# Pair 0 of the second layer's tail woven one step sooner with its operations held in order, and the last pair's bank copies put ahead of the softmax operations of the pair before it

## The chip, the cores and the metric

One core of one Trainium2 chip. The metric is device time in microseconds (us) of one execution, the median of several runs. Engines are called PE (TensorE, matrix products), DVE (VectorE), ACT (ScalarE), POOL (GpSimd) and SP (SyncE, here it only issues DMA). L937 is line 937 of the kernel before.

## The reference

Three stages, of which the last one carries the change:

```python
# stage 1: retention; x is 3072 tokens x 512
state = gamma * state + einsum('bhd,bhe->bhde', k[t], v[t])
y[t] = scale * einsum('bhd,bhde->bhe', q[t], state)
# stage 2: 512 -> 2048 -> 512
h = x @ w_in;  x = (h - tanh(h)) @ w_out
# stage 3: 512 -> 1024 -> 512
h = x @ w_in2
e = exp(h - max(h));  solu = h * e / (sum(e) + 1e-9)
ln = (solu - mean(solu)) / sqrt(var(solu) + 1e-6) * g_ln
return ln @ w_out2
```

## The kernel before, in words

Matrix products run on operands split into a high and a low part (`h`, `l`; `uh`, `ul` and so on): a 32-bit value is rounded to the format that PE takes at full rate (a cast on ACT), and the rest is what DVE or POOL get by subtraction. Each product is then three matmuls: high by high, high by low, low by high.

The end of stage 2 is a loop over `steps`, pairs (s, f): s counts six blocks of 512 tokens, f the 16 slices of 128 hidden features. Each step is 12 matmuls into four banks (`products_y`, L382), and two steps ahead of its use `split_p` casts the input `gp` on ACT (L165) and subtracts on DVE (L166). During the last block, s = 5, work of stage 3 for its first tokens is woven in between the steps.

Stage 3 takes 24 tiles of 128 tokens in 12 pairs. The first product of a pair, `h = x @ w_in2`, is done in seven block products instead of eight (`P1, P2, P6, P5, P7, P4, P3`, in this order; `Pair.part`, L1037): six matmuls each (`product2`, L930), with sums of the inputs made ahead (`sum_y` on POOL, `split_y`: casts `yha` and `yhs` on ACT, L508, subtractions `yla`, `yls` on POOL, L480). Some products add into a bank that an earlier one has filled, after the earlier sum has been copied out: P6 and P7 go on in P1's bank, P3 in P5's. `keep2` (L937, ACT) is that copy, four for each pair (after P1, P6, P5 and P7), and the bank can't be written on before the copy has been read out. `add_half` (L945, DVE) adds a bank and a kept copy into half a row of h and keeps the running minimum of -h.

Then for each half of the pair (`sa`, done first, and `sb`), class `Soft`: `exp` (L958, ACT), `weigh` (L964, DVE: h times e, and its mean), `center` (L970, ACT: less the mean), `turn` (L974, DVE: transposition in blocks, then a DMA to DRAM, L975) and `norm` (L980, ACT: Square with its sum, then small DVE and POOL operations). The function `turn(j)` reads both halves back with tokens and features exchanged (L992, SP). `high` (L999, ACT) and `low` (L1003, DVE) split that, and `outp` (L1015) makes the output tile: 24 matmuls, of which the first eight take `uh` alone, then a copy times the scale (L1028, ACT) and a DMA out. `outs(j)` does both tiles of pair j, tile 2j+1 (half a) first.

The order of PE in the tail is the program's own (`manual_schedule`). Other instructions are put in order by a scheduler, and those that pass through `fix` are held to the program's order once `late[0]` is true. Before the change that is so from the tail on; in the weave it is false. In the tail, pair j's seven products run (`pair_of`), and `high` and `low` of pair j-1 stand between the parts; for pair 1 they stand elsewhere (L1133 to L1166). Pair 10 is not followed by `outs`: its softmax runs, then its two `norm`, then pair 11's products, then the outputs of pairs 9, 10 and 11.

Of the kernel before, what the change touches and what calls it, by code (L numbers as in the profile page):

```python
# [43 lines left out]
NSB = NC  # L44
# [45 lines left out]
def body(ctx: ExitStack, tc, z, w_in, w_out, w_in2, w_out2, g_ln, cst, tab, out):  # L90
# [9 lines left out]
    def pin(ins, on=True):  # L100

        if on:
            tc.keep_in_program_order(ins)

    def t4(shape, dtype, name):
        return big.tile(shape, dtype, tag="t4", name=name)
# [51 lines left out]
    P1, P2, P6, P5, P7, P4, P3 = range(7)  # L158
    late = [False]

    def fix(ins):
        pin(ins, late[0])
# [303 lines left out]
    def step2(m):  # L466
        for st, n in enumerate((m + 3, m + 2, m + 1, m)):
            dec2.to(st, n)


    def load_y(j):
        t = t4([P, 2, NK, P], F32, "yl")
        nc.sync.dma_start(out=t, in_=y1d[j // 2][:, j % 2 * 2 : j % 2 * 2 + 2, :, :])
        yl[j] = t
# [196 lines left out]
    for n in range(NF1):  # L671
# [16 lines left out]
        else:  # L688

            dec1.n = 2 * NF1  # L690
            m = n - (NF1 - 4)
# [104 lines left out]
    def y_banks(s):  # L796
        at = [(ps_h, "h")] * 4 if s % 2 else [(ps_a, "r"), (ps_a, "r"), (ps_h, "h"), (ps_h, "h")]
        py[:] = [pool.tile([P, SB], F32, tag=tag, name="py") for pool, tag in at]

    def load_g(upto):  # L800
        while len(gs) < min(upto, len(steps)):
            s, f = steps[len(gs)]
            t = t2([P, SB], F32, "g")
            nc.sync.dma_start(out=t, in_=gd[s][:, f, :])
            gs[s, f] = t

    def split_p(n):
        w = t4([P, 2, SB], F32R, "gp")
        parts(w[:, 0, :], w[:, 1, :], gs[steps[n]], nc.vector)
        gp[n] = (w[:, 0, :], w[:, 1, :])  # L810
# [3 lines left out]
    def load_wo(upto):  # L814
        while len(wof) < min(upto, NF1):
            f = len(wof)
            wof[f] = t2([P, 512], F32, "wf")
            nc.sync.dma_start(out=wof[f], in_=wod[f])

    def split_wo(f):  # L820
        wo[f] = stage3(wof[f], None, nc.vector, False)
# [18 lines left out]
    for n in range(len(q) + 1):  # L840
        now, was = n < len(q), n > 0
        p, j = q[n] if now else (NSB, 0)
# [76 lines left out]
    def bank2():  # L919
        pool, tag = bank_of[0]  # L920
        bank_of.append(bank_of.pop(0))
        return pool.tile([P, 512], F32, tag=tag, name="ph2")

    def product2(j, m, ph, first=True):
        a = ys[j][m]
        n = 0
        for r in range(2):
            bh, bl = com.w[m, r]
            for x, w in ((a[0], bh), (a[0], bl), (a[1], bh)):
                nc.tensor.matmul(  # L930
                    ph, x[:, r, :], w, start=first and n == 0, stop=n == 5, skip_group_check=True
                )
                n += 1

    def keep2(ph):
        t = t2([P, 512], F32, "part")
        fix(nc.scalar.copy(t, ph))  # L937
        return t
# [4 lines left out]
    def add_half(h, half, ph, part, seen):  # L943
        hn, nm = h
        fix(nc.vector.tensor_tensor_reduce(  # L945
            hn[:, half * 512 : (half + 1) * 512], ph, part, -1.0,
            3.0e38 if seen is None else nm[seen], ALU.add, ALU.min, nm[half],
        ))

    class Soft:  # L950
# [21 lines left out]
        def turn(self):  # L972
            t = t4([P, FF2], F32, "ut")
            fix(nc.vector.transpose(t, self.hn))  # L974
            pin(nc.sync.dma_start(out=ud[self.i], in_=t))  # L975
            uc[self.i] = self.hn
# [20 lines left out]
    def high(i):  # L997
        uh, ul = ut[i] = [t4([P, NF2 * P], F32R, "u" + n) for n in "hl"]
        fix(nc.scalar.copy(uh, uc[i]))  # L999

    def low(i):
        uh, ul = ut[i]
        fix(nc.vector.tensor_tensor(ul, uc.pop(i), uh.bitcast(F32), ALU.subtract))  # L1003
# [27 lines left out]
    class Pair:  # L1031
# [5 lines left out]
        def part(self, m):  # L1037
            j = self.j
            if m == P1:
                self.q1 = bank2()  # L1040
                product2(j, P1, self.q1)
                self.kept = keep2(self.q1)
            elif m == P2:
                q = bank2()
                product2(j, P2, q)
                add_half(self.b, 0, q, self.kept, None)
            elif m == P6:
                product2(j, P6, self.q1, False)
                self.u2 = keep2(self.q1)
            elif m == P5:  # L1050
                self.q3 = bank2()
                product2(j, P5, self.q3)
                self.p5 = keep2(self.q3)
            elif m == P7:
                product2(j, P7, self.q1, False)
                self.kept = keep2(self.q1)
                add_half(self.a, 1, self.q1, self.p5, None)
            elif m == P4:
                q = bank2()
                product2(j, P4, q)  # L1060
                add_half(self.a, 0, q, self.kept, 1)
                self.sa = Soft(2 * j + 1, self.a, 0)
                self.sa.exp()
            else:
                product2(j, P3, self.q3, False)
                add_half(self.b, 1, self.q3, self.u2, 0)
                self.sb = Soft(2 * j, self.b, 1)
                self.sb.exp()
                ys.pop(j)

    bank_of = []
# [2 lines left out]
        nc.sync.dma_start(out=gd[s][:, f, :], in_=g)  # L1074
    for n, (s, f) in enumerate(steps):
        if n:
            if f == 0:
                y_banks(s)
                if s == NSB - 1:
                    bank_of[:] = [(ps_a, "r"), (ps_a, "r"), (ps_h, "h"), (ps_h, "h")]  # L1080
            load_g(n + 5)
            load_wo(n + 4)
            if n + 2 < len(steps):
                split_p(n + 2)
            if n + 2 < NF1:
                split_wo(n + 2)
            products_y(f, gp.pop(n), wo[f], py)
        if f == NF1 - 1:
            keep_y(s, py)
        if s >= NSB - 3 and n % 2 == 0 and com.n[2] < 12:  # L1090
            com.step()
        m = n - 2 * NF1 - 6
        if m >= 0 and m % 3 == 0:
            step2(m // 3)
        if s == NSB - 1:
            if f == 0:
                load_y(0)
            if f == 2:
                sum_y(0)
                load_y(1)  # L1100
            if f == 4:
                split_y(0)
            if f == 6:
                sum_y(1)
            if f == 9:
                load_y(2)
            if f == 8:
                pair = Pair(0)
            for m in {8: (P1, P2), 9: (P6, P5), 10: (P7, P4), 11: (P3,)}.get(f, ()):
                pair.part(m)  # L1110
                if m in (P4, P3):
                    u = pair.sa if m == P4 else pair.sb
                    u.weigh()
                    u.center()
                    u.turn()
                    u.norm()
            if f == 9:
                split_y(1)
            if f == 11:
                sum_y(2)  # L1120
            if f == 12:
                turn(0)
    G.close()
    M.close()

# [3 lines left out]
    NJ = NTT // 2  # L1129
# [3 lines left out]
    def pair_of(j, before=None):  # L1133

        a, b = (None, None) if before is None else (2 * before + 1, 2 * before)
        pair = Pair(j)
        for n, m in enumerate((P1, P2, P6, P5, P7, P4, P3)):
            pair.part(m)
            if n < 2 and j + 1 < NJ:
                split_y(j + 1, (n,))  # L1140
            if n == 2 and a is not None and j > 1:
                high(a)
                low(a)
            if n == 4:
                if a is not None:
                    if j > 1:
                        high(b)
                    else:
                        high(a)
                        low(a)  # L1150
                if j + 2 < NJ:
                    sum_y(j + 2)
                if j + 3 < NJ:
                    load_y(j + 3)
        for u in (pair.sa, pair.sb):
            u.weigh()
        if a is not None and j == 1:
            high(b)
        pair.sa.center()
        pair.sa.turn()  # L1160
        if a is not None:
            low(b)
        pair.sb.center()
        pair.sb.turn()
        turn(j)
        return pair  # L1166

    def outs(j, of=None, after=None):
# [8 lines left out]
    late[0] = True  # L1177
    with tc.manual_schedule(engines={mybir.EngineType.PE}):
        for j in range(1, NJ - 2):
            pair = pair_of(j, j - 1)  # L1180
            outs(j - 1, pair)
        pair = pair_of(NJ - 2, NJ - 3)
        pair.sa.norm()
        pair.sb.norm()
        pair = pair_of(NJ - 1)
        outs(NJ - 3, pair, NJ - 2)
        outs(NJ - 2, None, NJ - 1)
        outs(NJ - 1)
# [59 lines left out]
```

## Time and profile before

| | |
|---|---|
| three runs | 860.66 us median (860.16 to 861.43) |
| the profiled execution, its own time | 864.85 us |
| its span, first to last instruction | 863.1 us |
| PE busy | 823.6 us, 95% of the span |
| DVE, ACT, POOL busy | 64%, 55%, 36% |
| the weave of pair 0 (s = 5, f = 8 to 15) | 578 to 614.5 us |
| the tail, pairs 1 to 11 and all outputs | 614.5 to 860 us |
| mean granted clock of PE | 0.98 |

A busy PE is counted from modelled ends, so a matmul of 128x512 lasts 0.39 us in a row while the next one starts 0.227 us after it. In a timeline a row is a run of like instructions: start, duration, engine, line, operation, tiles, count, and in brackets how long the engine had been idle before it and what ended that.

### The profile page before, as it was taken

Reading aid. Unit: us, or ns where it says so; the run is one execution under the profiler, and the core shown is the slowest. Engines: PE = TensorE matmul, PEld = TensorE weight load, DVE = VectorE, ACT = ScalarE, POOL = GpSimd, SP = SyncE. Lnnn points to the kernel's source line nnn. Section 1 sums busy time; section 2 is a strip of 40 time slices with the busy share of each in tenths; the row PEclk is TensorE's granted clock in tenths of the full one; section 3 lists DMA queues with packets and bytes.
Section 4 is the critical chain, followed back from the end, with each engine's and each line's share of the span. In section 5 each row is a group of like instructions: output and inputs, shape, how many; then the busy total and the mean of one; then the engine's idle time right before and its main releaser. Section 6 shows DMA issues by size and latency. Waiting matters only on the chain.

```text
span 863.1 us, 16439 instructions
## 1 busy us (share of the span) xinstructions
PE 823.6 (95%) x6296; PEld 676.4 (78%) x6296; DVE 551.9 (64%) x1000; ACT 470.7 (55%) x880; POOL 309.0 (36%) x304
## 2 busy tenths in 40 slices
PE   4799999999999999999999999999899999999798
PEld 4678788788877777888888888887778888888686
DVE  3788875999856958232572888474466566565551
ACT  4555743656455546444571537254477677676652
POOL 4511200090534339443400260153545455455300
PEclk9799999999999999999999999999999999999999
DMA  9658753343898825964592718461877777777782
GB/s 360 251 198 308 260 197 131 122 175 122 301 363 303 304 76 170 403 256 142 199 373 86 285 57 302 140 233 37 160 146 147 147 147 147 161 165 142 128 147 62
DMA packets 168606, 169.43 MB, mean 196 GB/s; under 512 B 105680, under 2 KB 118224, under 8 KB 168528
## 3 DMA queue, kind: packets, MB, share of 16 engines
q1 hardware_dynamic: 160176, 153.51, 59.3%
q10 hardware_dynamic: 8352, 14.87, 4.9%
q8 instruction: 49, 0.80, 0.4%
q14 instruction: 29, 0.24, 0.1%
HBM read 107.02 MB, written 61.34 MB: 195 GB/s over the span
## 4 chain that ended last, share of the span: by engine, by line
PE 72%; DVE 11%; DMA 6%; issue 5%; ACT 4%; POOL 1%; SPq 1%; ACTq 0%; DVEq 0%; POOLq 0%
PE py L382 20%; PE po L1015 14%; PE ph L758 13%; PE ph L930 12%; PE ph L357 8%; DMA z<-z 3%; PE out L233 2%; PE sc L233 2%; DVE gl L373 1%; DVE wf L142 1%; DVE wf L145 1%; DVE w L155 1%; DMA raw<-w_in 1%; DMA gd<-hs 1%; DVE wf L139 1%
## 5 line engine op out<-in xcount | busy, mean ns | idle before, releaser
L382 PE MATMUL py<-gp,w 128*128 128x512 f32 x768 | 177.7, 392 | 2.5 <-ACT gp L165 2.1
L382 PEld LDWEIGHTS py<-gp,w 128*128 128x128 f32 x768 | 145.1, 189 | 34.1 <-ACT gp L165 2.8
L1015 PE MATMUL po<-w,uh 128*128 128x512 f32 x384 | 106.6, 389 | 0.0
L776 POOL TENSOR_TENSOR hs<-hs,th 128x512 f32<-128x512 f32 x48 | 66.7, 1393 | 95.6 <-ACT th L774 85.4
L1015 PEld LDWEIGHTS po<-w,uh 128*128 128x128 f32 x384 | 72.1, 188 | 15.0
L357 PE MATMUL ph<-xh,w 128*128 128x512 f32 x256 | 83.3, 400 | 0.1
L382 PE MATMUL py<-gh,w 128*128 128x512 f32 x256 | 79.2, 390 | 0.3 <-ACT gh L370 0.3
L154 ACT CAST w<-wf 128x512 fp32r<-128x512 f32 x70 | 43.0, 620 | 57.0 <-DVE wf L145 47.3
L930 PE MATMUL ph<-w,yhs 128*128 128x512 f32 x192 | 61.4, 402 | 4.9 <-ACT part L937 4.9
L1015 PE MATMUL po<-w,ul 128*128 128x512 f32 x192 | 63.1, 390 | 0.9 <-DVE ul L1003 0.9
L774 ACT ACTIVATE th<-hs 128x512 f32<-128x512 f32 x48 | 30.3, 632 | 61.2 <-DVE hs L784 54.7
L155 DVE TENSOR_TENSOR w<-wf,w 128x512 fp32r<-128x512 f32 x70 | 51.8, 745 | 14.5 <-ACT w L154 13.6
L166 DVE TENSOR_TENSOR gp<-g,gp 128x512 fp32r<-128x512 f32 x64 | 48.8, 774 | 19.1 <-ACT gp L165 19.0
L758 PE MATMUL ph<-xh,wch 128*128 128x512 f32 x140 | 56.9, 406 | 1.9 <-DVE hs L784 1.6
L945 DVE CUSTOM_DVE_ANT_0 hn<-ph,part 128x512 f32<-128x512 f32 x24 | 16.6, 692 | 64.9 <-ACT yha L508 41.5
L357 PEld LDWEIGHTS ph<-xh,w 128*128 128x128 f32 x256 | 48.6, 190 | 11.4 <-DVE w L155 0.6
L784 DVE TENSOR_TENSOR hs<-ph,part 128x512 f32<-128x512 f32 x48 | 33.0, 687 | 37.4 <-PE ph L758 24.0
L382 PEld LDWEIGHTS py<-gh,w 128*128 128x128 f32 x256 | 48.0, 188 | 10.6 <-ACT gh L370 0.7
L758 PE MATMUL ph<-xh,wcl 128*128 128x512 f32 x140 | 54.9, 392 | 1.1 <-issue 1.1
L165 ACT CAST gp<-g 128x512 fp32r<-128x512 f32 x64 | 38.6, 617 | 31.4 <-DMA g<-gd 21.4
L758 PE MATMUL ph<-xl,wch 128*128 128x512 f32 x140 | 54.9, 392 | 0.0
L758 PE MATMUL ph<-xh,wc 128*128 128x512 f32 x168 | 52.8, 390 | 0.3 <-ACT part L768 0.3
(125 smaller groups left out, 1794.1 us busy)
## 6 DMA issues: line engine op xcount, KB each, us to landing
z<-z SPq DMA_DIRECT2D x48, 512.0 KB, 7.1
g<-gd SPq DMA_DIRECT2D x64, 256.0 KB, 5.4
raw<-w_in SPq DMA_DIRECT2D x24, 512.0 KB, 6.6
raw<-w_out SPq DMA_DIRECT2D x24, 512.0 KB, 4.4
gd<-hs SPq DMA_DIRECT2D x48, 256.0 KB, 3.7
ud<-ut SPq DMA_DIRECT2D x24, 512.0 KB, 3.2
hn<-ud SPq DMA_DIRECT2D x24, 512.0 KB, 6.8
y1d<-ysb SPq DMA_DIRECT2D x24, 256.0 KB, 3.7
```

What stands on the lines that cost most here:

```text
L154: pin(nc.scalar.copy(hi, wf), fixed)
L155: pin(eng.tensor_tensor(lo, wf, hi.bitcast(F32), ALU.subtract), fixed)
L165: fix(nc.scalar.copy(h, src))
L166: fix(eng.tensor_tensor(o, src, h.bitcast(F32), ALU.subtract))
L233: pin(nc.tensor.matmul(o, a, b, start=True, stop=True, skip_group_check=True), held[0])
L357: nc.tensor.matmul(ph, a[:, k, :], x, start=n == 0, stop=n == 3 * NK - 1), s < 2
L382: nc.tensor.matmul(py[e], a[:, cols], x, start=f == 0 and n == 0, stop=f == NF1 - 1 and n == 2)
L758: nc.tensor.matmul(ph, a, x, start=first and n == 0, stop=n == 5, skip_group_check=True)
L776: eng.tensor_tensor(g, h, th, ALU.subtract)
L784: nc.vector.tensor_tensor(h, ph, part, ALU.add)
L930: nc.tensor.matmul(ph, x[:, r, :], w, start=first and n == 0, stop=n == 5, skip_group_check=True)
L1015: nc.tensor.matmul(po, a[:, f, :], dec2.w[f][lo], start=n == 0, stop=n == len(todo) - 1)
```

## The change

- In the last block, `late[0]` becomes true at f = 6, so what passes through `fix` is held in order from there.
- Pair 0's seven parts move from f = 8 to 11 to f = 7 to 10. Its softmax is no longer done half by half at once: at f = 10 stand weigh a, exp b, center a and turn a; at f = 11 weigh b, center b, turn b and the read-back; norm a at f = 12, norm b at f = 13. `exp` of half b leaves `Pair.part`.
- Pair 1 takes `high` and `low` of pair 0 at the same places as later pairs: half a behind P6, `high` of half b behind P7, `low` of half b behind its own turn a.
- The softmax of pair 10 is spread over the parts of pair 11: behind P1 weigh a, exp b, center a; behind P2 turn a, weigh b; behind P6 center b, turn b and the read-back; behind P5 norm a; behind P7 norm b. `low` of pair 9's half b moves ahead of pair 10's weigh.

```diff
@@ class Pair @@
                 self.sb = Soft(2 * j, self.b, 1)
-                self.sb.exp()
                 ys.pop(j)
@@ the loop over steps @@
         if n:
+            late[0] = late[0] or s == NSB - 1 and f == 6
...
-            if f == 8:
+            if f == 7:
                 pair = Pair(0)
-            for m in {8: (P1, P2), 9: (P6, P5), 10: (P7, P4), 11: (P3,)}.get(f, ()):
+            for m in {7: (P1, P2), 8: (P6, P5), 9: (P7, P4), 10: (P3,)}.get(f, ()):
                 pair.part(m)
-                if m in (P4, P3):
-                    u = pair.sa if m == P4 else pair.sb
-                    u.weigh()
-                    u.center()
-                    u.turn()
-                    u.norm()
+            if f == 10:
+                pair.sa.weigh()
+                pair.sb.exp()
+                pair.sa.center()
+                pair.sa.turn()
+            if f == 11:
+                pair.sb.weigh()
+                pair.sb.center()
+                pair.sb.turn()
+                turn(0)
+            if f == 12:
+                pair.sa.norm()
+            if f == 13:
+                pair.sb.norm()
             if f == 9:
                 split_y(1)
             if f == 11:
                 sum_y(2)
-            if f == 12:
-                turn(0)
@@ pair_of @@
-            if n == 2 and a is not None and j > 1:
+            if n == 2 and a is not None:
                 high(a)
                 low(a)
             if n == 4:
                 if a is not None:
-                    if j > 1:
-                        high(b)
-                    else:
-                        high(a)
-                        low(a)
+                    high(b)
...
+            yield n, pair
+        if j < NJ - 2:
+            pair.sb.exp()
+            pair.sa.weigh()
+            pair.sb.weigh()
+            pair.sa.center()
...
+        elif a is not None:
             low(b)
@@ the tail @@
-        pair = pair_of(NJ - 2, NJ - 3)
-        pair.sa.norm()
-        pair.sb.norm()
-        pair = pair_of(NJ - 1)
+        of = whole(NJ - 2, NJ - 3)
+        for n, pair in pair_of(NJ - 1):
+            if n == 0:
+                of.sa.weigh()
+                of.sb.exp()
+                of.sa.center()
+            elif n == 1:
+                of.sa.turn()
+                of.sb.weigh()
+            elif n == 2:
+                of.sb.center()
+                of.sb.turn()
+                turn(NJ - 2)
+            elif n == 3:
+                of.sa.norm()
+            elif n == 4:
+                of.sb.norm()
+        pair.sb.exp()
+        pair.sa.weigh()
...
         outs(NJ - 3, pair, NJ - 2)
```

Three places show how the built programs differ. The first is DVE in the weave, before (`ex_6793`, `hn_6686` are half a of pair 0, `ex_6844`, `hn_6689` half b; `gp_6814` is the input of f = 13, `gp_6868` that of f = 14):

```order
L974 STREAM_TRANSPOSE ut_6800<-hn_6686 128x1024
L983 TENSOR_SCALAR ssq_6803<-ssq_6803,ssum_6794 128x1
L984 TENSOR_SCALAR ssq_6803<-ssq_6803 128x1
L166 TENSOR_TENSOR gp_6814<-g_6709,gp_6814 128x512
L964 SCALAR_TENSOR_TENSOR ex_6844,us_6847<-hn_6689,ex_6844 128x1024
L981 TENSOR_SCALAR ssum_6845<-ssum_6845 128x1
L967 TENSOR_SCALAR us_6847<-us_6847 128x1
L982 RECIPROCAL ssum_6845<-ssum_6845 128x1
L974 STREAM_TRANSPOSE ut_6851<-hn_6689 128x1024
L983 TENSOR_SCALAR ssq_6854<-ssq_6854,ssum_6845 128x1
L984 TENSOR_SCALAR ssq_6854<-ssq_6854 128x1
L166 TENSOR_TENSOR gp_6868<-g_6759,gp_6868 128x512
```

and with the change (half a is `ex_6762`, `hn_6659`, half b `ex_6806`, `hn_6662`; `gp_6781`, `gp_6815`, `gp_6852` are the inputs of f = 12, 13, 14):

```order
L166 TENSOR_TENSOR gp_6781<-g_6682,gp_6781 128x512
L945 ISA hn_6662,nm_6664<-ph2_6717,part_6715,nm_6663 128x512
L945 ISA nm_6664 128x1
L964 SCALAR_TENSOR_TENSOR ex_6762,us_6803<-hn_6659,ex_6762 128x1024
L967 TENSOR_SCALAR us_6803<-us_6803 128x1
L964 SCALAR_TENSOR_TENSOR ex_6806,us_6838<-hn_6662,ex_6806 128x1024
L967 TENSOR_SCALAR us_6838<-us_6838 128x1
L974 STREAM_TRANSPOSE ut_6810<-hn_6659 128x1024
L166 TENSOR_TENSOR gp_6815<-g_6726,gp_6815 128x512
L974 STREAM_TRANSPOSE ut_6842<-hn_6662 128x1024
L166 TENSOR_TENSOR gp_6852<-g_6779,gp_6852 128x512
L981 TENSOR_SCALAR ssum_6763<-ssum_6763 128x1
```

The gp subtraction of f = 13 stood behind half a's whole chain and ahead of weigh b; now it stands behind both weighs and turn a, ahead of turn b, and the small operations of `norm` come after that of f = 14.

The second is ACT in the weave, before (names as above; `yha` and `yhs` are pair 1's inputs):

```order
L937 COPY part_6734<-ph2_6692 128x512
L937 COPY part_6743<-ph2_6736 128x512
L937 COPY part_6782<-ph2_6692 128x512
L958 ACTIVATE ex_6793,ssum_6794<-hn_6686,nm_6687 128x1024
L970 ACTIVATE hn_6686<-ex_6793,us_6796 128x1024
L980 ACTIVATE ex_6793,ssq_6803<-ex_6793,us_6796 128x1024
L165 CAST gp_6814<-g_6709 128x512
L958 ACTIVATE ex_6844,ssum_6845<-hn_6689,nm_6691 128x1024
L970 ACTIVATE hn_6689<-ex_6844,us_6847 128x1024
L980 ACTIVATE ex_6844,ssq_6854<-ex_6844,us_6847 128x1024
L165 CAST gp_6868<-g_6759 128x512
L165 CAST gp_6885<-g_6812 128x512
```

and now:

```order
L958 ACTIVATE ex_6762,ssum_6763<-hn_6659,nm_6660 128x1024
L508 CAST yha_6765<-yl_6541 128x512
L508 CAST yha_6765<-yl_6541 128x256
L508 CAST yhs_6772<-ysum_6637 128x1024
L165 CAST gp_6781<-g_6682 128x512
L958 ACTIVATE ex_6806,ssum_6807<-hn_6662,nm_6664 128x1024
L970 ACTIVATE hn_6659<-ex_6762,us_6803 128x1024
L165 CAST gp_6815<-g_6726 128x512
L970 ACTIVATE hn_6662<-ex_6806,us_6838 128x1024
L165 CAST gp_6852<-g_6779 128x512
L980 ACTIVATE ex_6762,ssq_6867<-ex_6762,us_6803 128x1024
L165 CAST gp_6876<-g_6813 128x512
```

The casts of gp stood behind exp, center and Square of a half; now one of them stands behind nearly every piece, and both Squares come last. Pair 1's three y casts moved behind exp a.

The third is ACT at the last pair, before (`ph2_8784` is the bank of P1, P6 and P7 of pair 11, `ph2_8809` that of P5 and P3; `ex_8730` and `ex_8740` are half a and b of pair 10):

```order
L958 ACTIVATE ex_8730,ssum_8731<-hn_8652,nm_8653 128x1024
L958 ACTIVATE ex_8740,ssum_8741<-hn_8655,nm_8657 128x1024
L970 ACTIVATE hn_8652<-ex_8730,us_8743 128x1024
L970 ACTIVATE hn_8655<-ex_8740,us_8746 128x1024
L980 ACTIVATE ex_8730,ssq_8760<-ex_8730,us_8743 128x1024
L980 ACTIVATE ex_8740,ssq_8769<-ex_8740,us_8746 128x1024
L937 COPY part_8791<-ph2_8784 128x512
L937 COPY part_8807<-ph2_8784 128x512
L937 COPY part_8816<-ph2_8809 128x512
L937 COPY part_8824<-ph2_8784 128x512
```

and now (the banks are `ph2_8747` and `ph2_8791`, half b is `ex_8759`):

```order
L958 ACTIVATE ex_8730,ssum_8731<-hn_8652,nm_8653 128x1024
L937 COPY part_8754<-ph2_8747 128x512
L958 ACTIVATE ex_8759,ssum_8760<-hn_8655,nm_8657 128x1024
L970 ACTIVATE hn_8652<-ex_8730,us_8756 128x1024
L937 COPY part_8783<-ph2_8747 128x512
L970 ACTIVATE hn_8655<-ex_8759,us_8774 128x1024
L937 COPY part_8798<-ph2_8791 128x512
L980 ACTIVATE ex_8730,ssq_8800<-ex_8730,us_8756 128x1024
L937 COPY part_8815<-ph2_8747 128x512
L980 ACTIVATE ex_8759,ssq_8818<-ex_8759,us_8774 128x1024
```

The four copies stood behind all six softmax operations of pair 10; now the first stands behind exp a alone, the second behind exp b and center a, the third behind center b, the fourth behind the first Square.

## Rows read from the trace of the kernel before

**Rows 1.** Waits of PE from 560 us to the end: engine, line, waited for, total us, times, longest.

```profile
PE ph L930 <- ACT part L937: 4.9, 1, 4.9
...
PE po L1015 <- DVE ul L1003: 0.9, 1, 0.9
```

**Rows 2.** Timeline of PE in the weave: start, us, engine, line, operation, count, idle before.

```profile
598.55 3.30 PE L382 MATMUL py<-gp,w 128*128 128x512 f32 x13
...
606.97 0.51 PE L382 MATMUL py<-gp,w 128*128 128x512 f32 x1 [2.06 <-ACT gp L165]
607.69 7.01 PE L382 MATMUL py<-gp,w 128*128 128x512 f32 x23 [0.22 <-DVE gp L166]
614.54 0.62 PE L930 MATMUL ph<-w,yha 128*128 128x512 f32 x2
```

**Rows 3.** Windows: stretch, busy of PE, PEld, DVE, ACT, POOL, then granted clock, DMA share, GB/s.

```profile
608.00:610.00 2.00, 2.00 (x6) 1.52 (x6) 1.38 (x2) 0.00 (x0) 1.42 (x3) 0.50 1.09 211
...
818.00:820.00 2.00, 2.00 (x6) 1.52 (x6) 0.37 (x2) 0.38 (x1) 0.00 (x0) 0.50 1.13 202
```

**Rows 4.** Timeline of ACT in the weave.

```profile
583.43 0.93 ACT L508 CAST yha<-yl 128x512 fp32r<-128x512 f32 x2
...
585.21 0.62 ACT L165 CAST gp<-g 128x512 fp32r<-128x512 f32 x1
...
595.57 1.15 ACT L958 ACTIVATE ex<-hn,nm 128x1024 f32<-128x1024 f32 x1 [1.67 <-DVE nm L945]
...
606.31 1.12 ACT L165 CAST gp<-g 128x512 fp32r<-128x512 f32 x2
```

**Rows 5.** Timeline of PE at the last pair.

```profile
808.86 0.62 PE L930 MATMUL ph<-w,yha 128*128 128x512 f32 x2
...
816.65 1.22 PE L930 MATMUL ph<-w,yhs 128*128 128x512 f32 x2 [4.91 <-ACT part L937]
...
826.36 1.98 PE L1015 MATMUL po<-w,uh 128*128 128x512 f32 x8
```

**Rows 6.** Timeline of ACT at the last pair.

```profile
808.60 1.15 ACT L958 ACTIVATE ex<-hn,nm 128x1024 f32<-128x1024 f32 x1 [0.28 <-DVE nm L945]
...
811.39 1.15 ACT L970 ACTIVATE hn<-ex,us 128x1024 f32<-128x1024 f32 x1 [0.23 <-DVE us L967]
...
816.03 0.56 ACT L937 COPY part<-ph 128x512 f32<-128x512 f32 x1
```

**Rows 7.** Timeline of DVE with POOL idle, in block s = 5 and at the last pair.

```profile
561.78 0.69 DVE L166 TENSOR_TENSOR gp<-g,gp 128x512 fp32r<-128x512 f32 x1 [0.62 <-ACT gp L165]
...
809.06 0.75 DVE L945 CUSTOM_DVE_ANT_0 hn<-ph,part,nm 128x512 f32<-128x512 f32 x1 [0.50 <-PE ph L930]
...
809.87 1.23 DVE L964 SCALAR_TENSOR_TENSOR ex<-hn,ex 128x1024 f32<-128x1024 f32 x1
...
811.21 1.22 DVE L964 SCALAR_TENSOR_TENSOR ex<-hn,ex 128x1024 f32<-128x1024 f32 x1
...
812.57 1.25 DVE L974 STREAM_TRANSPOSE ut<-hn 128x1024 f32<-128x1024 f32 x1
813.74 1.18 DVE L1003 TENSOR_TENSOR ul<-hn,uh 128x1024 fp32r<-128x1024 f32 x1
```

**Rows 8.** Timeline of DVE, with POOL at work, in the weave and in pair 2.

```profile
569.74 1.22 DVE L166 TENSOR_TENSOR gp<-g,gp 128x512 fp32r<-128x512 f32 x1
...
648.21 1.57 DVE L964 SCALAR_TENSOR_TENSOR ex<-hn,ex 128x1024 f32<-128x1024 f32 x1
...
649.88 1.24 DVE L974 STREAM_TRANSPOSE ut<-hn 128x1024 f32<-128x1024 f32 x1
```

**Rows 9.** The read-back's line (L992): issue to landing.

```profile
DMA to landing us min/median/max: 5.9/6.8/8.5
```

**Rows 10.** Timeline of PE and windows near 340 us.

```profile
340.76 0.50 PE L758 MATMUL ph<-xh,wch 128*128 128x512 f32 x1 [1.64 <-DVE hs L784]
...
341.00:345.00 4.00, 4.00 (x19) 3.27 (x19) 2.27 (x3) 2.42 (x5) 3.47 (x3) 1.00 0.84 284
```

More of the change, by code (lines that the diff above doesn't have):

```diff
@@ L1154, in pair_of, with whole @@
                     load_y(j + 3)
[L1155 to L1161, printed above, removed]
+            yield n, pair
[4 more added lines that the diff above has]
+            pair.sa.center()
+            pair.sa.turn()
+            if a is not None:
+                low(b)
+            pair.sb.center()
+            pair.sb.turn()
+            turn(j)
+        elif a is not None:
             low(b)
-        pair.sb.center()
-        pair.sb.turn()
-        turn(j)
+    def whole(j, before=None):
+        for _, pair in pair_of(j, before):
+            pass
         return pair
@@ L1179, in body @@
         for j in range(1, NJ - 2):
-            pair = pair_of(j, j - 1)
+            pair = whole(j, j - 1)
             outs(j - 1, pair)
-        pair = pair_of(NJ - 2, NJ - 3)
-        pair.sa.norm()
-        pair.sb.norm()
-        pair = pair_of(NJ - 1)
+        of = whole(NJ - 2, NJ - 3)
[17 more added lines that the diff above has]
+        pair.sa.weigh()
+        pair.sb.weigh()
+        pair.sa.center()
+        pair.sa.turn()
+        pair.sb.center()
+        pair.sb.turn()
+        turn(NJ - 1)
         outs(NJ - 3, pair, NJ - 2)
```

## The prediction

> **What bounds the kernel now.** I read the page first: TensorE (PE) is busy 95% of the span, so only the stretches where PE stands still or runs at half clock can give time back. The view of the waits of PE from 560 us to the end names them [rows 1, 2]: one wait of 4.9 us on a bank copy (L937), one of 2.1 on a gp cast (L165), one of 0.9 on a low part (L1003). I then read PE's timeline around each.
>
> The weave of pair 0 [rows 2]: step f=12 starts at 598.55. Twelve matmuls take 2.72 us at full clock (x23 would be 5.21), so the 48 matmuls of steps 12 to 15 should end 10.88 us later, at 609.43; pair 1 starts at 614.54. Lost: 5.11 us. Of that, 6.85 - 5.21 = 1.64 is half clock: the 23 matmuls from 607.69 take until 614.54, and the granted clock reads 0.50 there, the lower of its two levels (1.2 GHz) [rows 3]. The other 3.47 are waits. Their cause is ScalarE (ACT) [rows 4]: the gp casts for the next steps stand behind exp, center and Square of both halves, each of which waits for VectorE (DVE); the cast of f=14 starts at 606.31, when PE had been idle since 604.91 (606.97 less 2.06).
>
> The low part: 0.9 lost, in the second half of pair 0's outputs [rows 1].
>
> The last pair [rows 5]: its P1 starts at 808.86; a part (six matmuls) takes 1.36. P6 is due at 811.58 and starts at 816.65: 5.07 lost. The five parts from there should take 6.80 and take until 826.36, 9.71: another 2.91 lost at half clock [rows 3]. Together 7.98. The copy of P1's bank starts at 816.03, behind two exp, two center and two Square of pair 10 [rows 6], though P1 was done near 810.4.
>
> So 5.11 + 0.9 + 7.98 = 14.0 us is all that this change can reach. The profiled execution took 864.85 (span 863.1); the median of the three runs is 860.66, 4.19 lower. I make the sum against 864.85 and take the difference off the median.
>
> **The weave, pair 0 one step sooner.** No matmul is added or dropped, and f=12 still starts at 598.55, as five steps and seven parts stand before it either way. P3 and P4 come 2.72 sooner, and with them exp of half a: at 592.85 instead of 595.57 [rows 4]. Its 1.14, then the three y casts that stand behind it (1.78 together, yha at 583.43 to the next cast at 585.21 before), let the gp cast of f=12 start at 595.8; its DVE part ends at 597.1 to 597.7, due 598.78: hidden. Now the chain that decides, on DVE: add_half of P3 (0.75), weigh a, weigh b, turn a, and only then the gp subtraction of f=13, whose result PE needs at 601.50. With DVE alone a weigh costs 1.34 from start to start (809.87 to 811.21) and a turn 1.17 [rows 7]: add_half to 597.9, two weighs to 600.6, turn a to 601.8, the subtraction 0.69 (561.78), to 602.5: 1.05 late. With GpSimd (POOL) at work beside it a weigh costs 1.67 (648.21 to 649.88) and the subtraction up to 1.22, the turn no more (1.24 against 1.25) [rows 7, 8]: 598.4, 601.7, 602.85, 604.1: 2.6 late. POOL will be at work: y's low parts wait for the casts behind exp a, so they start at about 594.7, with the next sum behind them, and run beside this chain. I take a middle, 2.0 late, as POOL is shared out over the chain. The trace agrees in kind with the Trainium skill, "GPSIMD Engine Reference", section 1 (Specifications), which says that POOL's SBUF interfaces are shared with VectorE and collide with DVE instructions of two SBUF inputs; weigh and the subtraction have two, the turn has one. That rule speaks against this arrangement; left out, the wait would be 1.05 and the sum 0.95 lower. Steps 14 and 15 have slack: the subtraction of f=14 stands behind turn b and ends near 605.3, PE wants it at 606.2 by then. Gain: 5.11 - 2.0 = 3.1.
>
> SP's queue keeps its order of entries. The two reads of pair 0's turned halves issue behind turn b, which ends near 604.7 (603.5 plus its 1.17).
>
> **Pair 1's casts.** uh of half a moves to behind P6's copy and uh of half b to behind P7's, so ul of half b no longer waits behind exp and weigh. Pairs 2 to 9 have this order already, and the view of waits shows none of theirs [rows 1]. Gain 0.9; bounds 0 and 0.9. The cast now stands ahead of P5's copy, so that copy waits if the read-back is late: it lands 6.8 us after its issue, 8.5 at most [rows 9], so by 613.6 with an issue at 605.1, and the cast is due at 615.6 (P1 of pair 1 at 611.4, three parts and 0.2). Hidden.
>
> **The last pair.** Four copies move ahead of pair 10's softmax pieces; ul of half b also moves ahead of the first weigh on DVE. In the old clock of the trace: exp a 808.60, copy of P1 at 810.4, done 811.0, P6 due at 811.58: no wait. DVE: ul where weigh stood, 809.87 to 810.95 [rows 7]; weigh a, its mean at 812.35; center a 812.45; copy of P6 behind it 813.5 to 814.1, P7 due at 814.30: just in time. Turn a 813.65 to 814.8, weigh b, mean at 816.2, center b 816.3, copy of P5 817.35 to 817.95. P3 needs it at 817.02: 1.0 late. This stall is new. Were weighs at 1.67 and P6's copy late too, 1.9; with everything on time 0. POOL has no work there, so I keep 1.0. Behind it, Square a, copy of P7, Square b and the add_halves delay the last softmax; its Square ends near 828.5, the copy of outp(19) 829.2, the cast of uh(21) 829.6 to 830.6, and outp(21) is due at 830.25: 0.4 late (0 to 0.8). Loss after: 1.4 instead of 7.98. Gain 6.6. PE idle for 1.64 left the clock at its upper level, for 4.91 did not [rows 3, 5, 10], so half clock goes too.
>
> **Sum.** 3.1 + 0.9 + 6.6 = 10.6: 864.85 becomes 854.25 in the profiled terms, and 860.66 becomes **850.1**.
>
> **The rivals.**
> - *The clock falls at f=13* (0.30). PE waits of 1.64 idle left the clock at 1.00 [rows 10], of 2.06 did not [rows 2, 3]; 2.0 late is some 1.8 idle, between them. Price: as before, 1.64, so 851.7. For it: POOL beside both weighs. Against it: any chain nearer the DVE-alone bound.
> - *The cover is better than I think* (0.13): DVE-alone prices at f=13 (0.95 less), and half of the 1.4 at the end absorbed (0.7): 848.4.
> - *Slower: pair 1 waits for its read-back* (0.03). The cast of uh(1) stands ahead of P5's copy on ACT; if the read-back lands after 617.4 it delays P3 of pair 1 (due 619.5) microsecond for microsecond. To eat 10.6 it would have to land after 628, 23 us after its issue, where the longest in this trace is 8.5 [rows 9]. At 630 the time would be 862.7.
> - *No change* (0.03): the whole gain is taken back at the casts of uh(21) and uh(20), which stand behind the Squares and the copies of outp(19) and (18). The trace shows the cast of uh(21) waiting for nothing but its place; 10.6 us would need both read-backs late as well. Then 860.7.
>
> **Numbers.** Forecast 0.51 with 850.1. A measurement can tell some 0.2% (1.7 us) from no change. Best bounds together: weave 4.05, ul 0.9, last pair 7.5 (0.5 lost): 848.2. Worst without the last two rivals: weave 0.9 (2.6 late and half clock), ul 0, last pair 5.3: 854.5. Range for 8 in 10: 847.6 to 853.4. Faster 0.94 (forecast, clock, cover), same 0.03, slower 0.03.
>
> **What would show it.** Right: PE's waits lose the 4.9 on a copy and the 0.9 on ul; one wait of 1.5 to 2.2 on DVE's gp subtraction at the second matmul of f=13, where 2.1 on a cast stood; one near 1.0 on P5's copy in the last pair; pair 1 starts near 611.4. Half clock after f=13 speaks for the first rival. Wrong: a wait over 1.5 in the last pair, half clock there, a wait on a cast of uh in pair 1, or f=14 late as well.

## The result, and the profile after

| | before | after |
|---|---|---|
| median of four runs each | 860.41 us (858.77 to 861.43) | 850.78 us (848.72 to 851.22) |
| the profiled execution | 864.85 us | 848.72 us |
| its span | 863.1 us | 846.9 us |

The ratio is 0.9877, with a 95% interval of 0.9855 to 0.99. Forecast was 850.1 in a range of 847.6 to 853.4, and faster.

The two profiled executions differ by 16.1 us, more than the 9.6 us of the medians. Step f=12 of the weave starts at 598.55 before [rows 2] and at 593.45 after, so 5.1 us of the 16.1 lie ahead of everything that the change touches; the last section says what is known of them. All that follows is therefore counted from starts inside the weave and the tail.

Waits of PE from 545 us to the end, kernel after: engine, line, waited for, total us, times, longest.

```profile
PE py L382 <- DVE gp L166: 1.1, 1, 1.1
PE ph L930 <- ACT part L937: 0.7, 1, 0.7
PE py L382 <- ACT gp L165: 0.3, 1, 0.3
```

Against [rows 1], the 4.9 on a bank copy is 0.7 and the 0.9 on `ul` is gone. The 2.06 on a gp cast at f=14 [rows 2] is gone too, and f=13 now waits 0.3 for a cast and 1.1 for DVE's subtraction. Where PE waits in the weave, its timeline shows (start, us, engine, line, operation, tiles, count, idle before):

```profile
592.77 3.56 PE L382 MATMUL py<-gp,w 128*128 128x512 f32 x15
596.65 0.50 PE L382 MATMUL py<-gp,w 128*128 128x512 f32 x1 [0.32 <-ACT gp L165]
598.30 8.23 PE L382 MATMUL py<-gp,w 128*128 128x512 f32 x35 [1.14 <-DVE gp L166]
606.37 0.61 PE L930 MATMUL ph<-w,yha 128*128 128x512 f32 x2
```

The first row holds three matmuls of f=11 and twelve of f=12, which starts three times 0.227 after 592.77, at 593.45. Its 48 matmuls to the end of f=15 are due to be over 10.88 later, at 604.33; pair 1 starts at 606.37: 2.04 lost, where [rows 2] lost 5.11.

The last pair in PE's timeline, after:

```profile
799.48 0.62 PE L930 MATMUL ph<-w,yha 128*128 128x512 f32 x2
...
808.51 0.74 PE L930 MATMUL ph<-w,yhs 128*128 128x512 f32 x2 [0.70 <-ACT part L937]
...
810.02 2.00 PE L1015 MATMUL po<-w,uh 128*128 128x512 f32 x8
...
820.98 1.20 PE L1015 MATMUL po<-w,uh 128*128 128x512 f32 x4
```

P1 starts at 799.48, so P3, six parts of 1.36 later, is due at 807.64 and starts at 808.51; the outputs, due at 809.00, start at 810.02: 1.02 lost, all of it at P3. Two output tiles of 24 matmuls (5.44 each) put tile 21 at 820.90, and it starts at 820.98. So the last pair loses 1.10, where [rows 5] lost 7.98.

PE's clock right behind both of these waits, after (windows as in [rows 3]; the number behind the fifth engine is the granted clock):

```profile
598.00:602.00 4.00, 3.70 (x16) 3.09 (x17) 3.68 (x11) 3.58 (x7) 3.65 (x4) 1.00 0.76 222
810.00:814.00 4.00, 4.00 (x19) 3.29 (x18) 3.05 (x12) 2.75 (x6) 0.74 (x2) 1.00 1.19 229
```

It is 1.00, where [rows 3] read 0.50.

### The profile page after: what moved, and what is told of

The parts are those of the page before. It is cut to its first block, busy times and chain, and to the rows that moved or that the text cites. A ratio compares the mean times of both kernels' runs of the same rounds, so it can differ in the third digit from the quotient of the medians.

```text
span 846.9 us, 16439 instructions
## 1 busy us (share of the span) xinstructions
PE 816.8 (96%) x6296; PEld 672.5 (79%) x6296; DVE 552.9 (65%) x1000; ACT 470.4 (56%) x880; POOL 308.3 (36%) x304
## 4 chain that ended last, share of the span: by engine, by line
PE 83%; DVE 6%; DMA 4%; issue 3%; ACT 3%; POOL 1%; SPq 0%; ACTq 0%; DVEq 0%; POOLq 0%
PE py L382 29%; PE po L1015 15%; PE ph L758 14%; PE ph L930 12%; PE ph L357 8%; PE out L233 2%; PE sc L233 2%; DMA z<-z 1%; DMA raw<-w_in 1%; DMA wcd<-wch 1%; DMA wf<-wod 1%; DVE ex L964 1%; POOL hs L776 1%; DVE wf L139 1%; DVE wf L142 0%
## 5 line engine op out<-in xcount | busy, mean ns | idle before, releaser
L382 PE MATMUL py<-gp,w 128*128 128x512 f32 x768 | 175.6, 389 | 1.5 <-DVE gp L166 1.1
L930 PE MATMUL ph<-w,yhs 128*128 128x512 f32 x192 | 59.2, 390 | 0.7 <-ACT part L937 0.7
L382 PEld LDWEIGHTS py<-gh,w 128*128 128x128 f32 x256 | 48.0, 188 | 10.6 <-ACT gh L370 0.7
L1003 DVE TENSOR_TENSOR ul<-hn,uh 128x1024 fp32r<-128x1024 f32 x24 | 32.0, 1333 | 31.0 <-ACT uh L999 31.0
```

Source lines behind the costliest of these rows:

```text
L382: nc.tensor.matmul(py[e], a[:, cols], x, start=f == 0 and n == 0, stop=f == NF1 - 1 and n == 2)
L930: nc.tensor.matmul(ph, x[:, r, :], w, start=first and n == 0, stop=n == 5, skip_group_check=True)
```

## The experiments

The kernel before was measured again beside each group. It took 861.17 us (15 runs) beside the weave and pair 1 alone, the last pair alone, the order not held and pair 1's inputs split at f = 8; 861.57 (7 runs) beside pair 1's casts at their old places, the input of f=13, center b and all three; and 860.48 (11 runs) beside the last measurement. Each ratio is against its own group.

**The weave and pair 1 alone.** The last pair and pair 10's softmax stand as in the kernel before.

```diff
...
-        of = whole(NJ - 2, NJ - 3)
-        for n, pair in pair_of(NJ - 1):
...
+        pair = whole(NJ - 2, NJ - 3)
+        pair.sa.norm()
+        pair.sb.norm()
+        pair = whole(NJ - 1)
```

> Only the weave (with its hold) and pair 1's casts are changed; the last pair is as before. Theory (the parts add up, each loss is its own): PE waits in the weave as in the changed kernel (some 1.5 us at f=13, no half clock), none on ul in pair 1, and the old wait of 4.9 on a bank copy with half clock behind it. Time some 3 to 4.5 us under before, 856 to 857.5. Rival (the weave hands its gain to the last pair, or the other way round): within 1.5 us of before, or as fast as the whole change.

Measured: 856.85 us, ratio 0.9946 (0.9927 to 0.9965), 4.3 below before. Its waits of PE:

```profile
PE ph L930 <- ACT part L937: 4.9, 1, 4.9
PE py L382 <- DVE gp L166: 1.2, 1, 1.2
PE py L382 <- ACT gp L165: 0.3, 1, 0.3
```

The wait on `ul` and the half clock in the weave are gone; the 4.9 of the last pair stands at its old size, and half clock follows it again (window of the same profile):

```profile
811.00:813.00 2.00, 2.00 (x6) 1.59 (x5) 0.00 (x0) 0.59 (x1) 0.00 (x0) 0.50 1.50 188
```

**The last pair alone.** The weave and pair 1's casts stand as in the kernel before; the tail is that of the change.

```diff
-            late[0] = late[0] or s == NSB - 1 and f == 6
...
-            if f == 7:
+            if f == 8:
                 pair = Pair(0)
...
```

> Only the last pair is changed; the weave and pair 1 are as before. Theory: the waits of 2.1 on a gp cast, with half clock behind it, and of 0.9 on ul stand as before; the wait on a bank copy is 0.6 to 1.0 instead of 4.9, with no half clock. Time 6 to 7.5 us under before, 853 to 854.5. Rival (the copies were not the cause, the softmax chain behind them was): a wait of some us moves to the cast of uh for pair 10, and the gain is under 3.

Measured: 854.44 us, ratio 0.9911 (0.988 to 0.9941), 6.7 below before. Waits of PE:

```profile
PE py L382 <- ACT gp L165: 2.1, 1, 2.1
PE po L1015 <- DVE ul L1003: 0.9, 1, 0.9
PE ph L930 <- ACT part L937: 0.7, 1, 0.7
```

and a window behind the wait in the weave:

```profile
606.00:608.00 2.00, 2.00 (x6) 1.61 (x5) 0.00 (x0) 0.00 (x0) 0.00 (x0) 0.50 1.53 179
```

The weave is as it was, half clock too. So the two halves work in separate places: 4.3 and 6.7 make 11.0 beside 9.6 for the whole, and 10.5 in a second measurement of it (below), which the intervals cover.

**Pair 1's casts at their old places.** These are `high` and `low` of pair 0 (the expectation calls them bank copies; those are `keep2` and did not move here). Everything else is the change.

```diff
-            if n == 2 and a is not None:
+            if n == 2 and a is not None and j > 1:
                 high(a)
                 low(a)
...
```

> The change with pair 1's bank copies (high and low of pair 0) at their old places. Theory A (each idle stretch of TensorE in the trace of before is a term by itself, and they add): the wait of the o matmuls at L1015 on VectorE's ul, 0.9 us in before, comes back at its full size, the two weave waits of about 0.3 and 1.1 and the 0.7 before P3 stay; time 0.9 us above the change, about 851.7 (851.0 to 852.4). Theory C (the copies matter only where something else is late, so their place is worth nothing once the weave is on time): no wait over 0.2 us at L1015 in pair 1, and the time of the change within 0.4 us.

Measured: 851.99 us, ratio 0.9887 (0.9864 to 0.9909). Of its waits of PE one is not in the profile of the change:

```profile
PE po L1015 <- DVE ul L1003: 0.9, 1, 0.9
```

The wait is back at its full size: theory A. From pair 1's start to P1 of the last pair it takes 194.32 us here (608.38 to 802.70) and 193.11 in the change (606.37 to 799.48), so by starts the wait costs 1.21, more than its idle time. The medians alone would not have told, since the ratio's interval overlaps that of the change.

**The order not held in the weave.** The change without the line that holds the order from f = 6 on.

```diff
-            late[0] = late[0] or s == NSB - 1 and f == 6
```

> The whole change but for the hold: late stays false in the weave, so the scheduler orders its operations; pair 0 still runs one step sooner. Theory A (the hold matters: without it gp casts fall behind Squares again): PE waits over 1.5 us at f=13 or f=14, as before, time 1 to 4 us over the changed kernel. Theory B (the earlier step is what helps; the hold puts both weighs and a turn ahead of the subtraction of f=13 and costs): the scheduler puts that subtraction ahead of weigh b, the wait at f=13 shrinks from 1.5 to under 0.5, time 0.5 to 1.5 us under the changed kernel.

Measured: 850.71 us, ratio 0.989 (0.9861 to 0.9918). In its weave PE waits twice for a subtraction, 0.41 at f=12 and 0.32 at f=14, and from f=11's start to pair 1, 60 matmuls or 13.60, it loses 1.40, less than the 2.04 with the hold. DVE's timeline there:

```profile
590.92 1.23 DVE L964 SCALAR_TENSOR_TENSOR ex<-hn,ex 128x1024 f32<-128x1024 f32 x1 [1.31 <-ACT ex L958]
...
594.91 1.18 DVE L166 TENSOR_TENSOR gp<-g,gp 128x512 fp32r<-128x512 f32 x1
596.01 1.75 DVE L964 SCALAR_TENSOR_TENSOR ex<-hn,ex 128x1024 f32<-128x1024 f32 x1
```

Left free, the scheduler puts weigh a ahead of f=12's subtraction and weigh b behind it. The first weigh begins before POOL's work (591.48) and takes 1.23; the second begins beside it and takes 1.75. On ACT the gp cast of f=13 stands behind Square a again, as theory A says, but the waits that it expected do not come. Holding the order gave nothing. Without it the weave loses 0.6 us less by this trace, 0.3 of it is lost again at tile 21, whose cast PE waits for, and the medians show no difference. So the gain in the weave does not need the hold. It is put down to beginning a step sooner, which no run undid alone: in this kernel the pieces of the softmax also keep their new places in the program.

**Pair 1's inputs split at f = 8.** This takes POOL's work out from under the two weighs, and the three y casts from ahead of f=12's cast on ACT.

```diff
-            if f == 9:
+            if f == 8:
                 split_y(1)
```

> The whole change, with pair 1's y casts one step sooner (f=8), so that they stand ahead of exp a on ACT and POOL starts on the low parts some 3 us or more sooner. Theory (f=13 is late because POOL works beside both weighs, and because the gp cast of f=12 waits for the y casts): the weighs fall from 1.78 and 1.56 us to 1.2 to 1.4 each, the wait at f=13 from 1.5 to under 0.5; time 1 to 1.5 us under the changed kernel. Rival (the chain of exp, weigh and turn alone sets it): weighs shorter or not, the wait at f=13 stays over 1.0.

Measured: 847.82 us, ratio 0.9851 (0.9823 to 0.9878). DVE's timeline in its weave, the addition of P3 to the subtraction of f=13:

```profile
593.19 0.75 DVE L945 CUSTOM_DVE_ANT_0 hn<-ph,part,nm 128x512 f32<-128x512 f32 x1 [0.21 <-PE ph L930]
...
593.87 1.22 DVE L964 SCALAR_TENSOR_TENSOR ex<-hn,ex 128x1024 f32<-128x1024 f32 x1
...
595.32 1.22 DVE L964 SCALAR_TENSOR_TENSOR ex<-hn,ex 128x1024 f32<-128x1024 f32 x1
...
597.81 0.65 DVE L166 TENSOR_TENSOR gp<-g,gp 128x512 fp32r<-128x512 f32 x1
```

and POOL's, its last large operation ahead of them:

```profile
592.39 1.19 POOL L490 TENSOR_TENSOR ysum<-yl,ysum 128x256 f32<-128x256 f32 x1
```

and PE's, f=11 to f=15 in one row:

```profile
592.99 13.78 PE L382 MATMUL py<-gp,w 128*128 128x512 f32 x60
```

POOL is done at 593.58, both weighs take 1.22, and PE has no wait there: the theory, and more than the 1 to 1.5 us that it expected. Two things bring f=13's subtraction forward, against f=12. The addition of P3 starts 2.52 ahead of f=12 (593.19; f=12 is at 592.99 plus 2.72), where in the change it starts 1.26 ahead (592.19 and 593.45): 1.26 sooner, since f=12's subtraction is out of its way. And from weigh a to turn a it takes 2.78 (593.87 to 596.65) and not 3.57 (592.86 to 596.43): 0.79. Together 2.05, enough for the 2.04 that the weave lost. From 545 us to the end only the 0.7 in the last pair is left.

**The input of f=13 split one step sooner.**

```diff
+            early = s == NSB - 1 and f == 10
-            if n + 2 < len(steps):
+            if n + 2 < len(steps) and n + 2 not in gp:
                 split_p(n + 2)
+            if early:
+                split_p(n + 3)
```

> The change with the input of f=13 split one step sooner in the weave (at f=10), so its subtraction stands ahead of weigh b and turn a on VectorE. Theory A (VectorE's chain with weigh, weigh, turn in one stretch is what makes f=13 late, whatever the cause of its lengths): the wait of 1.1 us on VectorE's gp at f=13 goes, one of at most 0.5 may come at f=14; time 0.5 to 1.1 us below the change, about 850.0. Theory B (it is the whole chain of weigh a to turn b that is too long, and the wait only moves to the next input): 0.8 to 1.2 us of waits on gp stay at f=14 or f=15, and the time is that of the change.

Measured: 850.68 us, ratio 0.987 (0.9842 to 0.9898). Waits of PE:

```profile
PE py L382 <- DVE gp L166: 0.9, 1, 0.9
...
PE py L382 <- ACT gp L165: 0.4, 1, 0.4
```

Both now stand at f=14 (601.69 and 603.09, one step after the matmuls of f=13 ran on time). From f=11's start to pair 1, 1.89 are lost instead of 2.04. Theory B: it is the length of the chain on DVE that is late; changing which input stands behind it moves the wait by a step and keeps its size.

**Center b behind P5's copy.**

```diff
-            elif n == 2:
+            elif n == 3:
                 of.sb.center()
                 of.sb.turn()
                 turn(NJ - 2)
-            elif n == 3:
                 of.sa.norm()
```

> The change with the center and turn of pair 10's second token tile, and their read-back, moved behind P5's bank copy in the last pair, so that the copy is the next operation that ScalarE takes up. Theory A (the stall at P3 is P5's copy standing behind the center that waits for weigh b): the 0.7 us before P3 at L930 go. Theory B on what follows: the center leaves 0.6 us or more later, so the store, the read-back and the cast of uh(21) move with it and the o matmuls of tile 21, on time to 0.1 us in the change, wait 0.6 to 1.2 us at L1015: time that of the change to within 0.4 us, about 850.8. Rival: the read-back has slack, no wait over 0.3 us at L1015, and the time is 0.7 to 0.9 us below the change.

Measured: 850.93 us, ratio 0.988 (0.986 to 0.9901). The wait on the copy is gone, and in its place stands one that the change does not have:

```profile
PE po L1015 <- ACT uh L999: 0.8, 1, 0.8
```

Theories A and B held: the stall at P3 is the copy standing behind the center, and what is saved there is waited out at tile 21, whose cast stands behind the last pair's Square on ACT.

**All three.** The split at f = 8, center b behind P5's copy, and the last pair's norms behind the casts of tiles 21 and 20.

```diff
-            if of is not None:
+            if of is not None and after is None:
                 (of.sa if half else of.sb).norm()
             outp(2 * j + half)
             if after is not None:
                 high(2 * after + half)
                 low(2 * after + half)
+                if of is not None:
+                    (of.sa if half else of.sb).norm()
```

> Three edits on the change: pair 1's y split at f=8 of the weave, not 9; the center and turn of pair 10's second tile behind P5's bank copy; and the last pair's norms (ScalarE's Square and what follows) behind the casts of tiles 21 and 20, ahead of which they stood. Theory A (each wait is a term by itself): no wait over 0.4 us on TensorE from f=12 of the weave to tile 20's o matmuls; the casts of tile 21 are late by 0.4 us at most; time 0.4 to 1.0 us below the kernel with the y split alone (847.8), about 847.1 (846.3 to 848.0). Theory B (the last softmax's chain through the read-back sets the pace there, so a stall taken away ahead of it is waited out behind it): L1015 waits 0.6 us or more at tile 21 and the time is that of the y split alone.

Measured: 847.12 us, ratio 0.9833 (0.9813 to 0.9853). From 545 us to the end its view of PE's waits has no row. ACT's timeline in its last pair, P5's copy, center b, and the cast of tile 21:

```profile
804.43 0.59 ACT L937 COPY part<-ph 128x512 f32<-128x512 f32 x1 [0.49 <-PE ph L930]
806.15 1.15 ACT L970 ACTIVATE hn<-ex,us 128x1024 f32<-128x1024 f32 x1 [1.12 <-DVE us L967]
...
817.92 1.05 ACT L999 CAST uh<-hn 128x1024 fp32r<-128x1024 f32 x1 [0.41 <-ACT ob L1028]
```

The cast ends at 818.97 and the matmuls that read it start at 819.20, when they are due: on time, by some 0.2 us.

**The change and the two best versions, once more,** on one chip.

> The changed kernel once more, in five rounds, beside the two best versions: 850.7 (850.0 to 851.5). Its waits on TensorE after 550 us are the three of before (about 0.3, 1.1 and 0.7).

> The change with pair 1's y split at f=8, once more. If each wait taken away counts in full: 1.5 us of waits in the weave gone and up to 1 us more (the weave's f=12 to pair 1 was 2.0 late by starts), so 848.7 to 849.3; the first run of it was lower, 847.8. 848.4 (847.6 to 849.3).

> The version with all three edits (y split at f=8, the center behind P5's copy, the norms behind the casts), once more: by the 0.7 to 1.0 us of the stall at P3, below the y split alone, so 847.5 (846.8 to 848.2). If the last softmax's chain took the 0.7 back, it would stand within 0.3 us of the y split alone.

Measured: the change 850.01 us, ratio 0.9871 (0.9851 to 0.9891); the split alone 847.46, 0.9847 (0.9821 to 0.9874); all three edits 846.77, 0.9839 (0.9816 to 0.9863). The change has the same three waits as in its first profile. The split alone came out just under its range: its median is 2.5 us below the change's, where the rows of the weave show 2.04. The three edits together are the best version, 13.7 us below before. Their median is 0.7 below that of the split alone, but the intervals overlap, so only the trace shows that gain: from f=12 (593.61 and 593.53) to the end of the span (845.1 and 843.8) it takes 251.5 us with the split alone and 250.3 with all three.

## Why the prediction was right

**The weave** (forecast: 2.0 late at f=13 instead of 5.11 lost; measured 2.04). The place and the cause were as forecast. DVE's timeline, after, from the subtraction of f=12 to that of f=13:

```profile
591.31 0.96 DVE L166 TENSOR_TENSOR gp<-g,gp 128x512 fp32r<-128x512 f32 x1 [3.60 <-ACT gp L165]
592.19 0.74 DVE L945 CUSTOM_DVE_ANT_0 hn<-ph,part,nm 128x512 f32<-128x512 f32 x1
...
592.86 1.78 DVE L964 SCALAR_TENSOR_TENSOR ex<-hn,ex 128x1024 f32<-128x1024 f32 x1
...
594.76 1.56 DVE L964 SCALAR_TENSOR_TENSOR ex<-hn,ex 128x1024 f32<-128x1024 f32 x1
...
596.43 1.24 DVE L974 STREAM_TRANSPOSE ut<-hn 128x1024 f32<-128x1024 f32 x1
597.59 0.65 DVE L166 TENSOR_TENSOR gp<-g,gp 128x512 fp32r<-128x512 f32 x1
```

and POOL's beside it:

```profile
589.58 2.14 POOL L480 TENSOR_TENSOR yla<-yl,yha 128x256 fp32r<-128x256 f32 x3 [18.11 <-ACT yha L508]
591.68 5.23 POOL L480 TENSOR_TENSOR yls<-ysum,yhs 128x256 fp32r<-128x256 f32 x4
...
597.69 1.15 POOL L488 TENSOR_TENSOR ysum<-ysum,yl 128x256 f32<-128x256 f32 x1
```

The 2.0 was taken from between two bounds (1.05 and 2.6), and that it came out so near is in part luck. The weighs cost more than the bound with POOL at work: 1.90 and 1.67 from start to start, 3.57 where that bound had 3.34. The subtraction cost 0.65, not 1.22, though POOL was still at work: it began 0.10 ahead of POOL's sum at 597.69, and there the sum was the slower one (1.15; it takes 0.74 with DVE idle, at 590.99 of the kernel with the split at f = 8). Two sizes were off and offset each other. POOL's part of the loss is what the split at f = 8 takes off the weighs, 0.79 (forecast: 0.95). The other 1.26 is where the chain begins: the addition of P3 stands behind f=12's subtraction, that behind f=12's cast, and that behind three y casts on ACT. The forecast's times contained this (the cast of f=12 at 595.8, the addition of P3 done at 597.9), but its words called f=12's subtraction hidden. It is hidden for f=12, and not for what stands behind it on DVE, and this is the larger part of the 2.0.

This agrees with the rule that the prediction cited, the Trainium skill, "GPSIMD Engine Reference", section 1 (Specifications): shared SBUF interfaces, and collisions with DVE instructions of two SBUF inputs. Here weigh, with two inputs, takes 1.78 and 1.56 beside POOL, and 1.22 without; the turn, with one, takes 1.24 [rows 8] beside POOL and 1.25 without [rows 7].

The forecast did not name the 0.3 on ACT's cast of gp for f=13, which stands behind center a, and that behind the longer weigh a. It changes nothing in the sum, as the second matmul of f=13 waits later still.

**The clock at f=13** (a rival with 0.30: 1.64 more). It did not fall: the granted clock stayed 1.00 behind idle stretches of 0.32 and 1.14. The forecast of 1.8 idle in one piece was too long, and its sign of one wait of 1.5 to 2.2 did not show, since the 1.9 by which the second matmul was late came in two pieces with a matmul between. That PE's clock can fall in the weave is shown again by the kernel with the last pair alone, where 2.11 idle was followed by 0.50.

**Pair 1's casts** (0.9): the wait is gone after, and comes back with the old places. The 0.9 was the idle time of a row, counted from a modelled end, where the other two terms were taken from starts. From pair 1's start to P1 of the last pair it took 194.32 us before (614.54 [rows 2] to 808.86 [rows 5]) and takes 193.11 after: 1.21, so the term was 0.3 too small. The read-backs land in time, no wait on a cast of `uh` stands in pair 1.

**The last pair** (1.4 lost instead of 7.98; measured 1.10). ACT's timeline, after, has the stall as forecast:

```profile
804.07 0.57 ACT L937 COPY part<-ph 128x512 f32<-128x512 f32 x1
806.84 1.15 ACT L970 ACTIVATE hn<-ex,us 128x1024 f32<-128x1024 f32 x1 [2.20 <-DVE us L967]
807.89 0.56 ACT L937 COPY part<-ph 128x512 f32<-128x512 f32 x1
...
819.87 1.05 ACT L999 CAST uh<-hn 128x1024 fp32r<-128x1024 f32 x1 [0.41 <-ACT ob L1028]
```

P5's copy stands behind center b, which waits 2.20 for weigh b, and P3 is 1.02 late over all (forecast 1.0). The cast of tile 21 makes PE wait 0.08, not 0.4: of the last pair's terms that one alone was mis-sized.

**The sum.** By starts: 5.11 - 2.04 = 3.07 in the weave, 1.21 in pair 1, 7.98 - 1.10 = 6.88 in the last pair, 11.16 in all against a forecast of 10.6. From f=12 to the end of the span it is 863.1 - 598.55 = 264.55 before and 846.9 - 593.45 = 253.45 after, 11.1. The medians say 9.6 and, in the second measurement, 10.5. The change of 0.7 between the forecast 850.1 and the measured 850.78 is no larger than the difference of 0.8 between the two medians of the same kernel.

**The other rivals.** "The cover is better" (848.4) was half right at the end, by 0.3 of its 0.7, and wrong in the weave. A read-back late by 20 us, and a gain taken back wholly at the last casts, did not occur. The second has a true core, though: moving center b behind P5's copy takes 0.7 from P3 and gives 0.8 back at tile 21.

## What to carry to other kernels

When a chain of softmax pieces on one engine is laid beside matmul steps, add up everything on it between two due times, at the prices that hold with the neighbours at work; here an order chosen by hand, or an input made one step sooner, only chose which step waits, while moving what stands ahead of the chain on its feeding queues, and the neighbour's work beside it, took the wait away. A bank copy should not stand behind an operation that waits for a third engine, but look at what that operation feeds before putting it behind: here the saving came back as a wait until the next thing in that queue, a Square, had moved as well. A long idle stretch of TensorE is paid again where its clock falls behind it (4.91 idle and 2.91 at half clock here), so shortening it is worth more than the wait itself.

## What the runs showed of the hardware

The first part of the program differs from one execution to the next, for the same instructions. One difference is the clock. A window at 24 to 28 us of the kernel before:

```profile
24.00:28.00 4.00, 1.85 (x39) 1.47 (x33) 3.37 (x8) 2.23 (x9) 0.60 (x1) 0.50 1.03 398
```

and the same window of the kernel after, whose program is the same up to there:

```profile
24.00:28.00 4.00, 1.82 (x69) 1.64 (x61) 3.34 (x8) 2.24 (x9) 0.77 (x2) 1.00 1.03 396
```

PE is busy 1.8 us of 4 in both, at a granted clock of 0.50 in one (39 matmuls) and 1.00 in the other (69). The other difference is when the weave begins. The two profiled executions of the changed kernel, and the kernels with pair 1's old places and with center b moved, have the same instructions up to f=12; it starts at 593.45, 593.39, 595.46 and 596.25 in them. The clock is not the whole of this: the second execution of the changed kernel reads 0.55 at 17 to 20 us, where the first reads 1.00, and yet reaches f=12 as soon. What else makes the difference was not tried. Runs of one kernel spread by more than this document's smaller gains (before, here: 858.77 to 861.43; in the last measurement 858.18 to 864.08); that the late start is what spreads them is not shown. A gain under 1 us is better shown by a wait in the trace than by a median.

POOL is slowed as well as DVE: the four subtractions `yls` take 5.23 us beside the two weighs, 3.28 us where they run ahead of them, and 2.83 us in the kernel before, with DVE idle. In two places the operation that began first kept its time, and the other was the slower one: weigh a with the order not held (590.92, POOL from 591.48), and the subtraction of f=13 after. That this holds in general was not tried.
